# New durations and weights in the plan that orders a gated-attention and long-convolution kernel

## The chip, the core and the metric

The kernel runs on one core of a Trainium2 chip. The core has a matrix engine (TensorE, PE in the profile), a vector engine (VectorE, DVE), a scalar engine (ScalarE, ACT), a general engine (GpSimd, POOL) and a sync engine (SP), which here only issues transfers. Each engine takes its own instructions in the order in which the program has them and waits on semaphores for the others. The metric is the device time of one execution in microseconds (us); the median of the runs shown is what the change is held against.

## The reference

There are 8 batches of 3136 positions with 256 channels; `z` has 64 channels. Cut to what matters:

```python
scores = z @ z.T / S                    # S = 3136, per batch
attn = np.maximum(scores, 0.0) ** 2
x = u * (attn @ v)                      # 3136 x 256
x1, x2, x3 = split(x @ w_proj, 3)       # 256 channels each
X2 = rfft(x2, n=S); H = rfft(filter_fft, n=S)
y = x1 * irfft(X2 * H, n=S) * x3        # circular convolution along the positions
out = y @ w_out
```

So each batch has a squared-relu attention without a softmax, whose scores are symmetric, a gate `u`, three projections, a convolution over all 3136 positions by Fourier transform, a gate by `x1 * x3`, and a last projection.

## The kernel before

**The work of a batch.** The 3136 positions are 25 row tiles of 128 (the last has 64) and seven column chunks of 512, 512, 512, 512, 512, 256 and 320 (`CHUNKS`, line 24). For a chunk and a pair of row tiles, two score matmuls of 64 rows write the two halves of one of three pairs of PSUM banks (`ps_s`); they lie on the upper and the lower 64 rows of the array and run at the same time. ACT applies the relu (line 1672) into an SBUF tile `R_t`, DVE (line 1681) or ACT (line 1679) squares it into `A_t`, and "weighing" matmuls of 128 rows add `v` times `A_t` into two more banks, `ps_o0` and `ps_o1`, over all row tiles of the chunk. Since the scores are symmetric, the tiles of a later chunk are not computed twice: SP transposes them into `M` tiles (line 1610). When a chunk is done, DVE multiplies each of the two accumulators by `u` and the scale into `xT_t` (function `xe`, line 1722). That takes two instructions per accumulator, one for each half of 64 positions in a tile. The matmuls with `wp` then make `x1`, `x3` and `x2`; DVE's product of `x1` and `x3`, again in two instructions (`ev3`, line 1059), is kept as `gate_t`.

**The convolution.** A Fourier transform of 3136 = 64 x 49 points is made by matmuls in two stages with a trip through DRAM between them: `dft1` (line 889) writes `spec`, `load_spec` and `forward` read it again, DVE multiplies with the filter's transform `H`, `inverse` goes back through DRAM, and `add_end` (line 1224) does the last stage, the product with `gate_t` into `yT_t` (line 1252), the matmul with `wo`, a copy into `ost_t` and the store. This work of one batch is laid among the attention of the next.

**The plan.** No loop fixes the order of the instructions. The kernel makes a list of tasks, each with an estimated duration for every engine that may run it, its dependencies and the buffers it takes, and the class `Plan` (line 160) runs a clock over them: whichever engine can start a task first gets it, and the instructions are emitted in that order. Only the order reaches the chip; a task's estimated times do not. The estimates are `c_act`, `c_dve` and `c_pe` (lines 44 to 57), linear in the number of elements.

TensorE's tasks stand in queues: `S` for scores, `W` for weighing, `FA`, `FB` and `FZ` for projections, transforms and ends (called fill-in here). `pick_pe` (line 247) chooses. If scores are next and a run of them is already going, it goes on when the next pair of banks is free within `STAY`. Otherwise it wants two or three pairs free (three if the weighing that is ready is worth over `AMPLE`); while they are not, weighing may be taken, and fill-in too when the ready weighing is worth more than `BACKLOG` (line 29). Between weighing and fill-in a credit decides: each weighing task adds `PACE` (line 25), each fill-in task takes its duration away, and with a positive credit fill-in comes first, but only while `queued`, the work that ACT and DVE have waiting, is under `FULL` (line 37). The clock in `go` (line 309) adds a fixed time at every change from scores to other matmuls and back, since they use the array at different heights. For squares, `pick` (line 287) takes the engine that the clock says ends first, DVE being the first choice.

Of the kernel before, what the change touches and what calls it, by code (L numbers as in the profile page):

```python
# [21 lines left out]
KR = 2 * N2  # L22
KC = 100
CHUNKS = (512, 512, 512, 512, 512, 256, 320)
PACE = 0.6
HOLD = 3
DELAY = 4
GROUP = 1
BACKLOG, AMPLE, STAY = 2.0, 4.0, 0.1
LATE_PUT, LATE_LOAD, LATE_TURN, LATE_C, LATE_D2 = 3.0, 1.0, 1.5, 2.5, 1.0  # L30
SPEC_LAG = 1
LATE_F = 6.0
# [1 line left out]
FINAL = (0, 2, 4, 6, 1, 3, 5)  # L34
ZP, ZL = 0, 0.0
MOST = 3
FULL = 3.0
YIELD = 1.0
REACH = 2
INF = float("inf")  # L40
ISSUED = "issued"


def c_act(n):
    return 0.055 + n * 0.000833


def c_dve(n):
    return 0.068 + n * 0.00104
# [6 lines left out]
def c_pe(*ns):  # L56
    return sum(n / 2400 + 0.003 for n in ns)
# [102 lines left out]
class Plan:  # L160
# [86 lines left out]
    def pick_pe(self):  # L247
# [31 lines left out]
        order = ["S"]  # L279
        order += ["FA", "FB", "W", "FZ"] if self.credit > 0 and self.queued(t) < FULL else ["W", "FA", "FB", "FZ"]  # L280
        for k in order:
# [27 lines left out]
    def go(self):  # L309
        while True:  # L310
            got = []
            x = self.pick_pe()
            if x:
                got.append((x[0], 0, x[1], "PE", x[2]))
            for i, e in enumerate(self.pend):
                x = self.pick(e)
                if x:
                    got.append((x[0], i + 1, x[1], e, None))
            if not got:
                break  # L320
            start, _, task, e, k = min(got, key=lambda g: g[:2])
            if k:
                self.queues[k].remove(task)
                if (k == "S") != (self.mode == "S") and self.mode:
                    start += 0.11
                self.mode = k
                if k == "W":
                    self.credit = min(self.credit + PACE, 2.0)
                elif k != "S":
                    self.credit = max(self.credit - task.cost["PE"], -2.0)  # L330
            self.run(task, e, start)
        left = sum(len(q) for q in self.queues.values()) + sum(len(q) for q in self.pend.values())
        assert not left, f"{left} tasks left over"
# [3 lines left out]
def kernel(  # L337
# [60 lines left out]
    xT_p = Pool("xT", 8, [P, 2, 512], BF16)  # L398
# [93 lines left out]
    def on(engine, emit, cost, deps=(), takes=(), **kw):  # L492
        return job(None, lambda e: emit(), {engine: cost}, deps, takes, **kw)
# [13 lines left out]
    def both(n, first="ACT"):  # L507
        a, d = c_act(n), c_dve(n)
        return {"ACT": a, "DVE": d} if first == "ACT" else {"DVE": d, "ACT": a}
# [151 lines left out]
    for i, (t0, t1) in enumerate(zip(z_cuts, z_cuts[1:])):  # L661
        step_ = -(-(t1 - t0) // -(-(t1 - t0) // 8))
        for g0 in range(t0, t1, step_):
# [15 lines left out]
            n = nt * dqk  # L679
# [171 lines left out]
    for i0 in range(0, NS, 8):  # L851
        n = min(8, NS - i0)
# [170 lines left out]
    def add_proj(b, c, xt, xt_tasks):  # L1023
        cw = CHUNKS[c]
        users = []
        gtasks = []
        puts = []

        kind, late = ("FZ", 2) if b == B - 1 else ("FA", 0)

        def to_gates():
            for nb in range(2):
                box = {}

                def mm1(nb=nb, box=box):
                    box["p"] = bank()
                    box["x"] = x1_p.tile()
                    for k in range(2):
                        matmul(
                            box["p"][:, :cw], wp16[:, k, ds(nb * P, P)], xt["t"][:, k, :cw],  # L1040
                            start=(k == 0), stop=(k == 1),
                        )

                def ev1(e, box=box):
                    box["made"] = copy(e, box["x"][:, :cw], box["p"][:, :cw])

                def mm3(nb=nb, box=box):
                    box["p3"] = bank()
                    gates[b, c, nb] = g_p.tile()
                    for k in range(2):  # L1050
                        matmul(
                            box["p3"][:, :cw], wp16[:, k, ds((4 + nb) * P, P)], xt["t"][:, k, :cw],
                            start=(k == 0), stop=(k == 1),
                        )

                def ev3(nb=nb, box=box):
                    for h, w in halves(c):
                        g, p, x = (by_half(y, h, w) for y in (gates[b, c, nb], box["p3"], box["x"]))
                        got = nc.vector.tensor_tensor(g[:, ::-1] if h == 0 else g, p, x, ALU.mult)  # L1059
                        made.setdefault((b, c, nb), []).append(has_read(got, p, [box["made"]]))  # L1060

                a = pe(kind, mm1, c_pe(cw, cw), xt_tasks, [one_slots, x1_p.slots])
                if late and c in AFTER:
                    put_back.append(a)
                e1 = job(None, ev1, both(cw), [a], prio=late)
                e1.frees.append((a, 0))
                a3 = pe(kind, mm3, c_pe(cw, cw), [*xt_tasks, a], [one_slots, g_p.slots])
                e3 = on("DVE", ev3, c_dve(cw), [a3, e1], prio=late)
                e3.frees += [(a3, 0), (a, 1)]
                users.extend([a, a3])  # L1070
                gtasks.append((a3, e3))

        def to_spectrum():
            t0, n = T0[c], len(tiles[c])
            at = 0
            while at < n:
                nt = min(2, n - at)
                box = {}

                def mm2(at=at, nt=nt, box=box):  # L1080
                    box["p"] = bank()
                    box["x"] = x2_p.tile()
                    for k_ in range(nt):
                        for k in range(2):
                            matmul(
                                box["p"][:, ds(k_ * D, D)], xt["t"][:, k, ds((at + k_) * P, P)],
                                wp16[:, k, ds(D, D)], start=(k == 0), stop=(k == 1),
                            )

                def ev2(e, nt=nt, box=box):  # L1090
                    copy(e, box["x"][:, 0 : nt * D], box["p"][:, 0 : nt * D])

                a = pe("FA", mm2, c_pe(*[D] * (2 * nt)), xt_tasks, [one_slots, x2_p.slots])
                e2 = job(None, ev2, both(nt * D), [a])
                e2.frees.append((a, 0))
                users.append(a)
                puts.append(
                    dft1(
                        "FA", lambda box=box, nt=nt: box["x"][:, 0 : nt * D], t0 + at, nt, D1[b % 2],
                        [e2, t1_done], (a, 1), late=LATE_PUT * (b < B - 1),  # L1100
                    )
                )
                at += nt

        if b == B - 1 and c == NC - 1:
            to_spectrum()
            to_gates()
        else:
            to_gates()
            to_spectrum()  # L1110
        return users, puts, gtasks
# [225 lines left out]
    u_tasks = {}  # L1337
# [161 lines left out]
    w_first, w_last = {}, {}  # L1499
# [137 lines left out]
    for gi, g in enumerate(groups):  # L1637
        deps = []
        for un in g:
            b, c, k = un  # L1640
# [12 lines left out]
            for x in more:  # L1653
                weigh_short(*x)

        costs = [c_pe(CHUNKS[un[1]]) for un in g]
        extra = sum(c_pe(CHUNKS[c]) for _, c in more)
        st = pe("S", sg, sum(costs) + extra, deps, [pair_slots] * len(g))
        tails[gi] = st
# [1 line left out]
        for i, un in enumerate(g):  # L1661
            b, c, k = un
            cw = CHUNKS[c]
            pair = plans[b, c][k][1]
            rows, n = P, len(pair)
# [19 lines left out]
                "ACT", relu, c_act(n * cw), [(st, -sum(costs[i + 1 :]) - extra)], [R_p.slots], prio=0  # L1685
            )
            r_.frees.append((st, i))
            how = {"DVE": c_dve(n * cw)} if (b, c) == (0, 0) and k > 1 else both(n * cw, "DVE")
            q_ = job(None, sq, how, [r_], [A_p.slots], prio=1)
            q_.frees.append((r_, 0))  # L1690
            if c == NC - 1 and last or gi == len(groups) - 1:
# [15 lines left out]
            if last:  # L1707
                chunk_w[b, c] = [w_first[dh][0] for dh in range(2)], [w_last[dh] for dh in range(2)]
                xt = {}
                evs = []  # L1710
                for dh in range(2):

                    def xe(dh=dh, b=b, c=c, cw=cw, xt=xt):
                        if dh == 0:
                            xt["t"] = xT_p.tile()
                            if cw % P:
                                nc.vector.memset(xt["t"][:, :, cw : cw + N1], 0.0)
                        for h, n in halves(c):
                            x, f = by_half(xt["t"][:, dh], h, n), by_half(full[b, c, dh], h, n)
                            ut = uT[b, c][:, 0:n, dh, ds(h * N1, N1)]  # L1720
                            x = x[:, ::-1] if h == 0 else x
                            nc.vector.scalar_tensor_tensor(x, f, inv_s2, ut, ALU.mult, ALU.mult)  # L1722

                    x_ = on(
                        "DVE", xe, c_dve(cw), [w_last[dh], u_tasks[b, c], *((d, ISSUED) for d in evs)], [xT_p.slots] if dh == 0 else [], prio=-1
                    )
                    evs.append(x_)
                    x_.frees.append(w_first[dh])
# [45 lines left out]
    for gi, got in ends_at.items():  # L1774
        for b, c in got:
            q_, un, _ = short[b, c]
# [39 lines left out]
```

## Time and profile before

| | us |
|---|---|
| median of 3 runs | 1019.09 |
| lowest and highest run | 1015.51, 1020.16 |
| the profiled execution | 1017.42 |
| its span, first to last instruction | 1015.6 |
| PE busy | 980.1 (97%) |
| ACT busy | 882.6 (87%) |
| DVE busy | 821.6 (81%) |
| POOL busy | 188.3 (19%) |

The granted clock of TensorE was 0.998 over the span. The costliest groups are ACT's relus, 528 with 473.0 us; the weighing matmuls, 2128 with 480.4 us; DVE's squares, 334 with 366.5 us; and ACT's squares, 194 with 184.4 us. In the profile's lists of groups a row gives line, engine, operation, output and input tiles with their shapes, the count, then busy time and mean duration, and after the second bar the idle time of the engine just before these instructions and what ended it. In the timeline a row begins with its start and its length; equal neighbours are merged, and a bracket tells of idle time before the first. Matmuls overlap, because each is recorded from its issue to its modelled end; their starts say more than their lengths.

### The profile page before, as it was taken

To read this page: it belongs to the slowest core of one execution; us is meant where nothing else is said; L and a number is where in the kernel's file an instruction comes from. 1 tells how busy PE (TensorE), PEld (TensorE's weight loads), DVE (VectorE), ACT (ScalarE), POOL (GpSimd) and SP (SyncE) were. 2 spreads that over 40 slices of the span, in tenths; PEclk is the share of its full clock that TensorE was granted. 3 is DMA by queue.
4 is the path that set the end of the run, shared out by engine and by line. 5 is a ranking of instruction groups with operands and counts; after the bars stand their busy time and mean duration, and the time that the engine had idled before them with its cause. 6 is when DMAs were issued, how large, how long until landed. Compare 5 with 4: busy or idle time off the path is not lost. (4 is left out here: it accounts for less than half of the span.)

```text
span 1015.6 us, 17745 instructions
## 1 busy us (share of the span) xinstructions
PE 980.1 (97%) x6046; PEld 493.1 (49%) x6046; DVE 821.6 (81%) x1440; ACT 882.6 (87%) x1247; POOL 188.3 (19%) x401
## 2 busy tenths in 40 slices
PE   6999999999999999999999999999999999999986
PEld 2344644446444554445544464444644455544664
DVE  7977779877789787897789878887788977898674
ACT  5877899987989889888999898999888989998884
POOL 5142311123111310222012131112201132000000
PEclk9999999999999999999999999999999999999999
DMA  9699878888678799888988789696888979978756
GB/s 169 127 181 171 157 137 147 170 177 184 139 155 171 139 181 207 163 151 149 208 187 167 140 182 210 129 186 133 179 193 155 191 130 170 213 165 172 126 183 210
DMA packets 331770, 170.18 MB, mean 168 GB/s; under 512 B 241160, under 2 KB 306504, under 8 KB 331680
## 3 DMA queue, kind: packets, MB, share of 16 engines
q1 hardware_dynamic: 303952, 138.09, 63.0%
q0 software_dynamic: 27728, 30.97, 20.8%
q8 instruction: 47, 0.77, 0.3%
q14 instruction: 43, 0.35, 0.1%
HBM read 90.26 MB, written 53.35 MB: 141 GB/s over the span
## 5 line engine op out<-in xcount | busy, mean ns | idle before, releaser
L1672 ACT ACTIVATE R_t<-ps_s 128x1024 f32<-128x1024 f32 (+3 forms) x528 | 473.0, 932 | 71.0 <-PE ps_s L465 52.9
L465 PE MATMUL ps_o_t<-A_t,v_t 128*128 128x512 bf16 (+4 forms) x2128 | 480.4, 355 | 4.1 <-DVE A_t L1681 3.3
L1681 DVE TENSOR_TENSOR A_t<-R_t 128x1024 bf16<-128x1024 f32 (+3 forms) x334 | 366.5, 1114 | 113.0 <-ACT R_t L1672 112.2
L465 PEld LDWEIGHTS <-v_t 128*128 128x128 bf16 (+1 forms) x2826 | 253.5, 98 | 265.0 <-issue 65.3
L1679 ACT ACTIVATE A_t<-R_t 128x1024 bf16<-128x1024 f32 (+4 forms) x194 | 184.4, 955 | 2.5
L465 PE MATMUL ps_s<-zT_t 64*128 64x512 bf16 (+2 forms) x1064 | 152.6, 356 | 4.1 <-ACT s_t L498 1.7
L548 POOL COPY tick<-xT_t 1x1 bf16<-1x1 bf16 x54 | 13.8, 256 | 729.3 <-DVE xT_t L1722 713.2
L465 PE MATMUL ps_s<-xT_t,wp 128*128 128x512 bf16 (+2 forms) x430 | 102.6, 352 | 2.7 <-DVE xT_t L1722 1.3
L498 ACT ACTIVATE x_t<-ps_s 128x512 bf16<-128x512 f32 (+2 forms) x148 | 79.6, 573 | 25.4 <-PE ps_s L465 17.7
L1722 DVE SCALAR_TENSOR_TENSOR xT_t<-ps_o_t,uT_t 128x256 bf16<-128x256 f32 (+2 forms) x224 | 76.3, 382 | 21.3 <-PE ps_o_t L465 16.4
L465 PEld LDWEIGHTS <-zT_t 64*128 64x128 bf16 (+1 forms) x1081 | 44.8, 95 | 97.0 <-issue 78.6
L1158 DVE TENSOR_TENSOR xh<-xh,H 100x1024 bf16<-100x1024 bf16 x120 | 80.9, 685 | 3.0 <-ACT xh L498 2.2
L465 PE MATMUL ps_o_t<-M_t,v_t 128*128 128x512 bf16 (+2 forms) x352 | 82.2, 353 | 0.0
L1059 DVE TENSOR_TENSOR gate_t<-ps_s,x_t 128x256 bf16<-128x256 f32 (+2 forms) x214 | 71.1, 383 | 12.9 <-PE ps_s L465 11.0
L465 PEld LDWEIGHTS <-wp 128*128 128x128 bf16 x448 | 42.5, 97 | 45.7 <-issue 8.9
L539 POOL DMA_DIRECT2D un_t<-in_u_dram x112 | 59.9, 557 | 9.8 <-issue 5.7
L1252 DVE TENSOR_TENSOR yT_t<-ps_s,gate_t 128x512 bf16<-128x512 f32 (+2 forms) x97 | 58.2, 623 | 3.1 <-PE ps_s L465 2.6
L558 POOL DMA_DIRECT2D v_t<-in_v_dram x112 | 59.5, 554 | 6.0 <-issue 1.7
L465 PE MATMUL ps_s<-wp,xT_t 128*128 128x256 bf16 x398 | 56.4, 272 | 0.4 <-DVE gate_t L1059 0.2
L465 PE MATMUL ps_s<-wo,yT_t 128*128 128x256 bf16 (+1 forms) x366 | 54.2, 273 | 1.3 <-DVE yT_t L1252 0.9
L498 ACT ACTIVATE s_t<-ps_s 128x512 bf16<-128x512 f32 (+1 forms) x79 | 45.2, 587 | 9.4 <-PE ps_s L465 4.3
L498 ACT ACTIVATE xh<-ps_s 100x512 bf16<-100x512 f32 (+1 forms) x90 | 51.8, 611 | 1.6 <-PE ps_s L465 1.4
(148 smaller groups left out, 842.3 us busy)
## 6 DMA issues: line engine op xcount, KB each, us to landing
out_dram<-ost_t SPq DMA_DIRECT2D x66, 256.0 KB
spec<-s_t SPq DMA_DIRECT2D x96, 128.0 KB
spec_in_t<-spec SPq DMA_DIRECT2D x28, 392.0 KB
spec<-gs_t SPq DMA_DIRECT2D x28, 392.0 KB
v_t<-in_v_dram POOLq DMA_DIRECT2D x80, 128.0 KB, 4.1
un_t<-in_u_dram POOLq DMA_DIRECT2D x80, 128.0 KB, 4.5
conv_in_t<-spec SPq DMA_DIRECT2D x33, 256.0 KB
out_dram<-ost_t SPq DMA_DIRECT2D x19, 128.0 KB
```

Source lines behind the costliest of these rows:

```text
L465: wrote(nc.tensor.matmul(o, *args, **kw), o)
L498: got = nc.scalar.activation(out_, in_, AF.Copy)
L539: nc.gpsimd.dma_start(out=t[ds(j * N1, N1), lo - t0 : hi - t0, :], in_=x[:, n2 : n2 + hi - lo, :])
L548: nc.gpsimd.tensor_copy(tick[:], xt["t"][0:1, 1, 0:1])
L558: nc.gpsimd.dma_start(out=t[ds(j * N1, N1), ds(v_at(a), (b - a) * D)], in_=r[:, n2 + a - lo : n2 + b - lo, :].rearrange("p t d -> p (t d)"),)
L1059: got = nc.vector.tensor_tensor(g[:, ::-1] if h == 0 else g, p, x, ALU.mult)
L1158: nc.vector.tensor_tensor(x[:, 1 - i], x[:, 0], h, ALU.mult)
L1252: got = nc.vector.tensor_tensor(yb["y"][:, dh, 0:w], p, gates[b, c, dh][:, 0:w], ALU.mult)
L1672: has_read(nc.scalar.activation(blocks(box["R"], n, cw)[:rows], p, AF.Relu), p)
L1679: nc.scalar.activation(a, r, AF.Square)
L1681: nc.vector.tensor_tensor(a, r, r, ALU.mult)
L1722: nc.vector.scalar_tensor_tensor(x, f, inv_s2, ut, ALU.mult, ALU.mult)
```

## The change

Durations: the estimate of a DVE product of two instructions, for `xT` and for the gates, rises by 0.064 us. A square on ACT rises by 0.039. Each score matmul rises by 0.008. The time added at a change between scores and other matmuls falls from 0.11 to 0.095. Weights: `PACE` falls from 0.6 to 0.55 and `BACKLOG` from 2.0 to 1.0, and `FULL` becomes infinite, so that the condition on `queued` always holds. `INF` moves up in the file, and lines behind it stand one further down. The instructions themselves are written as before.

```diff
+INF = float("inf")
-PACE = 0.6
+PACE = 0.55
-BACKLOG, AMPLE, STAY = 2.0, 4.0, 0.1
+BACKLOG, AMPLE, STAY = 1.0, 4.0, 0.1
-FULL = 3.0
+FULL = INF
...
                 if (k == "S") != (self.mode == "S") and self.mode:
-                    start += 0.11
+                    start += 0.095
...
-                e3 = on("DVE", ev3, c_dve(cw), [a3, e1], prio=late)
+                e3 = on("DVE", ev3, c_dve(cw) + 0.064, [a3, e1], prio=late)
...
-        costs = [c_pe(CHUNKS[un[1]]) for un in g]
+        costs = [c_pe(CHUNKS[un[1]]) + 0.008 for un in g]
...
-            how = {"DVE": c_dve(n * cw)} if (b, c) == (0, 0) and k > 1 else both(n * cw, "DVE")
+            how = {"DVE": c_dve(n * cw)} if (b, c) == (0, 0) and k > 1 else {"DVE": c_dve(n * cw), "ACT": c_act(n * cw) + 0.039}
...
-                        "DVE", xe, c_dve(cw), [w_last[dh], u_tasks[b, c], *((d, ISSUED) for d in evs)], [xT_p.slots] if dh == 0 else [], prio=-1
+                        "DVE", xe, c_dve(cw) + 0.064, [w_last[dh], u_tasks[b, c], *((d, ISSUED) for d in evs)], [xT_p.slots] if dh == 0 else [], prio=-1
```

More of the change, by code (lines that the diff above doesn't have):

```diff
@@ L36 @@
 MOST = 3
-FULL = 3.0
+FULL = INF
 YIELD = 1.0
 REACH = 2
-INF = float("inf")
 ISSUED = "issued"
```

## The prediction

> **What bounds the kernel now.** I read the page's first two parts, then the timeline of TensorE alone, then the waits, then the stretches of time, and last the timeline around the final load of the spectrum.
>
> ```profile
> PE 980.1 (97%) x6046; PEld 493.1 (49%) x6046; DVE 821.6 (81%) x1440; ACT 882.6 (87%) x1247; POOL 188.3 (19%) x401
> PE   6999999999999999999999999999999999999986
> ```
>
> TensorE (PE) is busy in every slice but the first and the last two. "Busy" says little of pipelined matmuls, so I go by their starts:
>
> ```profile
> 499.56 1.89 PE L465 MATMUL ps_o_t<-A_t,v_t 128*128 128x512 bf16 x8
> 501.39 0.82 PE L465 MATMUL ps_s<-zT_t 64*128 64x512 bf16 x6
> 502.14 1.04 PE L465 MATMUL ps_o_t<-A_t,v_t 128*128 128x512 bf16 x4
> ```
>
> Eight matmuls of 512 columns begin at 499.56 and the next group at 501.39, 1.83 us later; an undisturbed matmul of 512 columns follows the one before it after 0.215 us (the commonest interval in this timeline; 0.109 for 256 columns, 0.135 for 320, 0.055 for 128), so eight are 1.72, and about 0.1 is left over. The six score matmuls are 64 rows high and run two at a time: three times 0.215 is 0.645, the next group begins 0.75 after them, and again 0.1 is left. That remainder, 0.095 in the median, stands at every change between matmuls of 64 and of 128 rows. With these intervals the built order of before needs 909.1 us of streaming and 404 changes x 0.095 = 38.4. Before the first matmul lie 4.7 us and after the last one 8.1. Together that is 960.3 of the span's 1015.6; 55.3 us are waits: 8.8 in the first 25 us, 10.2 in the last 50, some 36 in between. **So the end is set by TensorE's order and by its small waits**, and no other engine has a share to give.
>
> ```profile
> PEld L465 <- DVE xT_t L1722: 11.9, 25, 1.1
> PE ps_o_t L465 <- DVE A_t L1681: 3.3, 8, 0.6
> PE ps_o_t L465 <- DVE xT_t L1722: 2.1, 5, 0.8
> PE ps_s L465 <- ACT s_t L498: 2.0, 2, 1.7
> PE ps_s L465 <- DVE gate_t L1059: 1.4, 4, 0.7
> ```
>
> Columns: who waits for whom, us in all, times, longest. The largest of these is the product that makes `xT` (two DVE instructions at L1722): the weight loads stood 11.9 us for it, the matmuls themselves, whose modelled ends cover a part, 2.1 here. By starts it is between: 7.2.
>
> ```profile
> 30.00:955.00 925.00, 912.73 (x5581) 452.76 (x5580) 758.90 (x1298) 826.63 (x1154) 174.64 (x368) 1.00 0.85 167
> 967.00:974.40 7.40, 6.41 (x59) 4.39 (x58) 6.12 (x15) 4.83 (x9) 0.00 (x0) 1.00 0.48 141
> ```
>
> Stretches: length, then busy time of PE, weight loads, DVE, ACT and POOL, granted clock, DMA. In the body ACT works 826.6 of 925 us and DVE 758.9: neither is full, and the clock is 1.00.
>
> ```profile
> 966.59 0.49 PE L465 MATMUL ps_s<-x_t,T 128*128 128x512 bf16 x2
> ...
> 969.86 0.34 SPq L928 DMA_DIRECT2D spec_in_t<-spec  x1
> ...
> 973.73 0.90 PE L465 MATMUL ps_s<-wo,yT_t 128*128 128x256 bf16 x4 [0.45 <-DVE yT_t L1252]
> 974.46 0.60 PE L465 MATMUL ps_s<-spec_in_t,S 98*100 98x256 bf16 x4
> ```
>
> At the tail the last first-stage transform (966.59) is copied, stored, loaded again (issue 969.86) and used at 974.46: 7.9 us of transfers, which fill-in matmuls worth 5.8 us cover in part.
>
> **The change part by part.** The 6046 matmuls stay the same; five instructions net go from DVE to ACT. What changes is the order that the plan makes, so I compare the two built orders.
>
> (1) Balance. DVE gets 7 more squares of 1024 columns (1.220 us each) and ACT 7 fewer (1.068), ACT 16 more `gs_t` copies (0.613) and DVE 16 fewer (0.685); with the smaller moves, each at its row's mean, ACT gains 1.4 us and DVE loses 3.1, of 882.6 and 821.6. On engines that are not full I take nothing; bounds -1.4 and +1.4.
>
> (2) Start. TensorE's order is the same up to its first 21.4 us of work, which in the trace ends near 35.9 us; ACT's first 27 and DVE's first 73 instructions are the same. The 8.8 us of waits of the first 25 us stay: 0.
>
> (3) Changes of height: 426 instead of 404. 22 x 0.095 = +2.1 us, all of it on TensorE. The Trainium skill, page "TensorEngine Tiling (Array Packing)", section "Key Properties", says that a change of tiling mode drains TensorE; that speaks against this change, and the 0.095 at each change agrees with it. By the 166 ns that its page "TensorE: Matmul & The Clock Gate", section "Single matmul latency", gives as the fixed part of a lone warm matmul, the term would be +3.7 and the forecast 1.6 us later, as an estimate; the row is this kernel's own and decides.
>
> (4) Tail. In the changed order 4.3 us of fill-in stand between that last transform and the first use of the spectrum, not 5.8: eight matmuls of 512 columns (projections to gates, 8 x 0.215 = 1.7) now stand ahead of the transform, two of 256 columns moved in (0.2). The wait is one of transfers (issue at 969.86, use 4.6 us later), so work moved ahead of it delays the whole tail: +1.5. Bounds: 0, if the fill-in had itself been late (its last group waited 0.45 for `yT`), and +1.7. Behind it the order of all engines has the same steps, and the distances to the final loads are equal (5.4 us at the least in both).
>
> (5) Waits in the body. For every result that TensorE needs from ACT or DVE I took the distance in the built order: matmul work, at the intervals above and 0.095 per change, between the last matmul that fed it and the first that needs it, or that overwrites the bank. Short distances wait. For each kind I chose the length at which the shortfalls of the old order add up to the wait measured in the trace by starts (intervals over 25 ns too long, 40 to 955 us: 25.0 in all), and took the new order's shortfalls at the same length:
> `xT` to the projections, 0.96 us: 2.8 becomes 1.7. `xT` to the next chunk's accumulators, 1.33: 4.5 becomes 0.8. Gates (L1059), 1.23: 1.4 to 0.6. DVE squares, 2.84: 2.5 to 1.1. ACT squares, 3.54: 0.9 to 2.4. Relu to other work on its bank, 1.33: 3.7 to 2.8; to scores, 1.79: 0.3 to 1.3. ACT copies to scores, 1.28: 4.7 to 5.9; to other work, 0.99: 1.0 to 1.2. DVE copies, 1.12: 1.4 to 2.2. `yT`: 0.0 to 0.2. Together 23.2 becomes 20.2: -3.0.
> This fits the edit: products of two instructions get 0.064 us more in the plan (0.600 to 0.664 for 512 columns, where the trace has 2 x 0.417 and in the timeline 0.75 for both), so they are asked for later. What is late next are ACT's copies ahead of scores, since with `BACKLOG` at 1.0 scores and fill-in crowd more. ACT squares were short at two places only, so their length is the least certain; without them the term is -4.5. Bounds: -9.6 (all waits for `xT`, gates and ACT squares go) and +5, from the same stretch: as many waits as came off `xT` and the gates come back on copies.
>
> No transfer in the body comes nearer: a mirrored tile is used 12.2 us of work or more after its scores before, 12.9 after; a spectrum of an earlier batch 14.9 and 13.8, where the tail's wait shows that 7.9 are enough.
>
> Sum: 2.1 + 1.5 - 3.0 = +0.6. The profiled execution took 1017.42 us (span 1015.6, 1.8 around it), so 1018.0. That execution lies 1.7 below the median of 1019.09 and inside 1015.51 to 1020.16; about 0.5%, 5 us, is what a measurement of this kernel can tell from none.
>
> **The rivals.**
> Better match. If a plan whose durations are the chip's loses not single waits but a general mistrust, half of the 25.0 us go: -12.5 + 2.1 + 1.5 = -8.9, 1008.5. For it: four durations that are corrected (squares on ACT, two-instruction products, score matmuls, 0.110 to 0.095 per change) stand at 9.6 us of waits. Against: distances to copies and relus, two fifths of the waits, aren't longer in the new order.
> Other waits, as many. The order is redrawn and the body's waits remain 25: 1017.4 + 2.1 + 1.5 = 1021.0. For it: the waits lie evenly, about 0.4 us in 10; against: `xT`'s distances are clearly longer.
> Bunching, the slower one. `FULL` at infinity takes away the brake that held back projections, spectra and ends while ACT and DVE had over 3 us of work queued. With the rows' durations laid where their inputs are ready in the order, the mean load of ACT and DVE exceeds a stretch of 10 us by 7.4 us in all before and by 15.5 after (40 to 900 us of TensorE's work). If each such excess becomes a wait, +8.1: 1026.1. Against: the worst stretch holds 11.8 us of work in 10, 1.8 too much, while the median weighing stands 6.7 us behind its scores and needs 2.8, so 3.9 are in reserve. It decides from where excesses adjoin and pass 3.9.
> No effect. The new values might have left the order as it was; but it differs from TensorE's 22nd us on.
>
> **How the numbers follow.** Forecast 1018.0, chance 0.45, own range 1013 to 1023. Better match 0.20. Redrawn 0.17. Bunching 0.18. Against 1019.09, faster by over 0.5% is below 1014.0: nearly all of the better match and a tenth of the forecast, 0.25. Slower is above 1024.2: most of the bunching and a little of the forecast and of the redrawn, 0.19. Same: 0.56. The range 1009 to 1026 reaches almost to both outer cases and holds the bounds of (3) to (5) but their last ends.
>
> **What would show it.** In the changed kernel's waits, weight loads standing for `xT` should fall from 11.9 to near 6, and `ACT` copies ahead of score matmuls should not fall; the interval at a change of height stays 0.095; between the last `x_t,T` and the first `spec_in_t,S` there are still 7.5 to 8 us, with TensorE idle for some 3.5 instead of 2. I'm wrong if the sum of waits in the body leaves 18 to 28 us, if DVE has stretches full for 20 us with TensorE standing behind squares, or if the tail's wait shrinks.

## The result and the profile after

The changed kernel takes 1021.06 us in the median of 13 runs (1019.16 to 1026.08), the kernel before 1017.42 in the median of as many on the same chip: a ratio of 1.0036, 95% interval 1.0022 to 1.0049. It is 3.7 us slower. (The three runs shown before the prediction had a median of 1019.09; the ten added ones brought it down by 1.7.) The time lies in the predicted range, 3 us above the forecast of 1018.0; but the forecast was no change that could be seen, and the change is a loss. The profiled execution after took 1019.36 us, its span is 1017.6; it is among the quickest of the 13.

The page of the changed kernel, its busy time per engine and, in 40 slices, TensorE's busy share and granted clock:

```profile
PE 975.4 (96%) x5957; PEld 493.6 (49%) x6046; DVE 820.0 (81%) x1435; ACT 884.1 (87%) x1252; POOL 189.0 (19%) x401
...
PE   6999999999999999999999999999999999999985
...
PEclk9999999999999999999999999999999999999998
```

89 of the 6046 matmul records are missing here, so PE's busy time is not smaller than before; the weight loads are complete. ACT gained 1.5 us and DVE lost 1.6, and neither is fuller in any way that counts. New is the 8 at the end of the clock.

The waits of the changed kernel, first of weight loads, then of matmuls, then of ACT (who waits for whom, us in all, times, longest):

```profile
PEld L466 <- DVE xT_t L1723: 8.2, 21, 0.7
...
PE ps_s L466 <- ACT ost_t L499: 2.7, 4, 1.1
PE ps_s L466 <- ACT x_t L499: 2.5, 7, 0.4
...
ACT ost_t L499 <- DMA out_dram<-ost_t: 4.7, 4, 1.9
```

`xT` costs less, 8.2 instead of 11.9, as the new estimate of its product would have it. The last line is the one that grew most: ACT stood four times, 4.7 us in all, at a copy into an output buffer `ost_t` until a store of that buffer had landed. In the trace before that happened once, for 1.1 us. TensorE's waits for those copies are the 2.7 us above them.

What one such wait looks like. First ACT in the changed kernel, then the chain of what released it (start, us, what):

```profile
725.07 1.94 ACT L1673 ACTIVATE R_t<-ps_s 128x1024 f32<-128x1024 f32 x2 [0.44 <-PE ps_s L466]
727.28 0.60 ACT L499 ACTIVATE ost_t<-ps_s 128x512 f32<-128x512 f32 x1 [0.27 <-DMA out_dram<-ost_t]
729.78 1.08 ACT L499 ACTIVATE ost_t<-ps_s 128x512 f32<-128x512 f32 x2 [1.90 <-DMA out_dram<-ost_t]
730.75 1.95 ACT L1673 ACTIVATE R_t<-ps_s 128x1024 f32<-128x1024 f32 x2
```

```profile
721.40 0.28 SPq L1312
...
721.73 7.94 DMA out_dram<-ost_t
...
```

The copy at 727.28 is the only one of the short chunk of 256, the next the first of another chunk. That one could have begun at 727.9; it began at 729.78, when a store issued at 721.7 had landed, 7.9 us after its issue. ACT works in order, so the relu at 730.75 is late too, and with it the score banks. The same happens 122 us earlier, in the batch before. The SP queue shows why the store was out so late; first the changed kernel, then the kernel before at the same place of its batch:

```profile
594.42 0.53 SPq L941 DMA_DIRECT2D conv_in_t<-spec  x1
595.05 1.18 SPq L1392 DMA_TRANSPOSE zT_t<-zd_t  x1
596.39 1.97 SPq L1348 DMA_TRANSPOSE uT_t<-un_t  x1
598.45 2.70 SPq L1312 DMA_DIRECT2D out_dram<-ost_t  x4
...
608.14 1.11 SPq L1312 DMA_DIRECT2D out_dram<-ost_t  x2
```

```profile
600.09 1.20 SPq L1311 DMA_DIRECT2D out_dram<-ost_t  x2
604.39 0.37 SPq L903 DMA_DIRECT2D spec<-s_t  x1
604.88 1.75 SPq L1311 DMA_DIRECT2D out_dram<-ost_t  x2
...
610.69 1.12 SPq L1311 DMA_DIRECT2D out_dram<-ost_t  x2
```

Before, the stores of three chunks go out in pairs 4.8 and 5.8 us apart. In the new order two chunks end close together (their `wo` matmuls begin at 592.6 and 595.5). The first one's copies are done at 594.5, but its stores stand behind a load and two transposes until 598.4, and both chunks' four stores leave in one row. At 604.4 the third and the fourth chunk come, 12 `wo` matmuls in one group, and need both buffers again. The last of the four stores lands 6.9 us after its issue here (600.57 to 607.41) and 7.9 in the next batch, and the fourth chunk's copy waits for it. The plan counts 3.8 us from issue to landing on a free bus (1.2 + 4 x 0.45 + 0.8, from its constants), so it took both chunks to be free of any wait. That is about the usual time: each store marks its landing in the trace by 16 semaphore updates, and by these the median of the 92 stores is 3.7 us before and 3.6 in the changed kernel. Single stores take up to 8.1 and 8.4; the pairs of the kernel before that are shown above took 4.4 and 5.3, 3.5 and 4.0. By the Trainium skill, page "DMA: Bandwidth & Descriptors", section "Anatomy of one DMA — SWDGE (gpsimd) path", a transfer issued by GpSimd takes about 2.0 us and its bytes at 436 GB/s, which as an estimate makes 3.2 us for the 512 KB of a chunk. These stores are issued by SP and were not alone; the trace has 6.9 and 7.9 here, and decides.

The tail, TensorE in the changed kernel (start, us, line, operation, idle before):

```profile
966.77 0.49 PE L466 MATMUL ps_s<-x_t,T 128*128 128x512 bf16 x2
...
974.21 0.81 PE L466 MATMUL ps_s<-spec_in_t,S 98*100 98x256 bf16 x5 [0.35 <-ACT ost_t L499]
...
976.17 0.42 PE L466 MATMUL ps_o_t<-un_t,S 98*100 98x512 bf16 x1 [0.72 <-DMA un_t<-spec]
...
977.59 0.85 PE L466 MATMUL ps_s<-xh,TZ 100*98 100x256 bf16 x3
```

and stretches of the changed kernel (length, then busy time of PE, weight loads, DVE, ACT and POOL, granted clock, DMA share, GB/s):

```profile
967.00:974.40 7.40, 5.86 (x56) 4.01 (x55) 5.06 (x12) 4.55 (x9) 0.00 (x0) 1.00 0.44 129
974.02:977.43 3.41, 2.09 (x11) 1.02 (x11) 1.44 (x3) 2.99 (x8) 0.00 (x0) 1.00 0.81 226
977.40:980.80 3.40, 3.37 (x14) 2.86 (x14) 2.20 (x4) 1.56 (x3) 0.00 (x0) 0.50 1.01 387
```

The trip of the spectrum is no longer than before (966.77 to 974.21 is 7.4 us, 7.9 before). Then the clock drops to 0.50 for 3.41 us: the three matmuls of 256 columns at 977.59 take 0.64 us until the next group instead of 0.33.

### The profile page after: what moved, and what is told of

It reads as the page before. It is cut to its first block, busy times and chain, and to the rows that moved or that the text cites. A ratio compares the mean times of both kernels' runs of the same rounds, so it can differ in the third digit from the quotient of the medians.

```text
span 1017.6 us, 17693 instructions
## 1 busy us (share of the span) xinstructions
PE 975.4 (96%) x5957; PEld 493.6 (49%) x6046; DVE 820.0 (81%) x1435; ACT 884.1 (87%) x1252; POOL 189.0 (19%) x401
## 4 chain that ended last, share of the span: by engine, by line
PE 75%; DVE 10%; ACT 6%; DMA 5%; issue 3%; SPq 1%; ACTq 0%; DVEq 0%
PE ps_o_t L466 43%; PE ps_s L466 32%; DVE A_t L1682 3%; ACT R_t L1673 3%; DMA out_dram<-ost_t 2%; DVE xh L1159 2%; ACT A_t L1680 1%; ACT x_t L499 1%; DVE x_t L503 1%; DVE gate_t L1060 1%; DVE xT_t L1723 1%; DMA un_t<-spec 1%; DMA ost_t<-in_z_dram 1%; DVE yT_t L1253 0%; DMA A_t<-spec 0%
## 5 line engine op out<-in xcount | busy, mean ns | idle before, releaser
L466 PE MATMUL ps_o_t<-A_t,v_t 128*128 128x512 bf16 (+4 forms) x2061 | 471.9, 354 | 9.9 <-DVE A_t L1682 3.0
L1682 DVE TENSOR_TENSOR A_t<-R_t 128x1024 bf16<-128x1024 f32 (+3 forms) x341 | 373.1, 1111 | 107.4 <-ACT R_t L1673 106.5
L466 PEld LDWEIGHTS <-v_t 128*128 128x128 bf16 x2826 | 253.7, 98 | 261.2 <-issue 67.6
L1680 ACT ACTIVATE A_t<-R_t 128x1024 bf16<-128x1024 f32 (+3 forms) x187 | 177.8, 957 | 2.5
L466 PE MATMUL ps_s<-zT_t 64*128 64x512 bf16 (+2 forms) x1064 | 155.3, 357 | 5.6 <-ACT ost_t L499 2.4
L499 ACT ACTIVATE gs_t<-ps_s 98x512 bf16<-98x512 f32 (+1 forms) x99 | 59.1, 617 | 3.4 <-PE ps_s L466 3.1
L499 ACT ACTIVATE xh<-ps_s 100x512 bf16<-100x512 f32 (+1 forms) x93 | 54.1, 618 | 2.0 <-PE ps_s L466 1.8
L466 PE MATMUL ps_s<-wo,yT_t 128*128 128x256 bf16 (+1 forms) x358 | 51.7, 273 | 1.3 <-DVE yT_t L1253 0.9
```

Of the source, the lines that this page charges most:

```text
L466: wrote(nc.tensor.matmul(o, *args, **kw), o)
L499: got = nc.scalar.activation(out_, in_, AF.Copy)
L1680: nc.scalar.activation(a, r, AF.Square)
L1682: nc.vector.tensor_tensor(a, r, r, ALU.mult)
```

## The experiments

Two measures are used. "Body waits" is the sum of step (5) of the prediction: intervals between matmul starts over 25 ns too long, from 40 to 955 us; it is given where the trace has all its matmul records. "Last 50 us" is the account of all waits there. Ratios are against the kernel before, run on the same chip beside them.

**Four runs on where the loss sits.** They were made before the output buffers were suspected; their theories put the loss into the tail, its clock, or bunched work.

```diff
# dur_only: the new durations, the old weights
-PACE = 0.55
+PACE = 0.6
-BACKLOG, AMPLE, STAY = 1.0, 4.0, 0.1
+BACKLOG, AMPLE, STAY = 2.0, 4.0, 0.1
-FULL = INF
+FULL = 3.0
# weights_only: the kernel before with the three new weights
# late_old: the changed kernel; from the last batch's first scores on
...
+            if g[0][0] == B - 1:
+                PACE, BACKLOG, FULL = 0.6, 2.0, 3.0
# warm_after: the changed kernel with 8 more matmuls in the tail's gaps
+                    for _ in range({0: 3, 4: 3}.get(j, 0) if final else 0):
+                        matmul(box["p"][:, :], ident[:, :], wp16[:, 0, 0:512], start=True, stop=True)
...
+                        for _ in range(2 if final and j == 0 else 0):
+                            matmul(box["p"][:, :], ident[:, :], wp16[:, 0, 0:512], start=True, stop=True)
```

> The corrected durations alone, with the old weights 0.6, 2.0 and 3.0. Built order: 426 changes of height; the last first-stage transform ends at 910.2 us of TensorE's work, and 9.4 us of fill-in follow, more than the 7.7 us that the transfers take. Distances in the body give 20.7 us of waits against 23.1 before. Theory A: the tail starts only 0.3 us later than before and stays filled, so 0.3 - 2.4 = -2.1 us, ratio 0.998, with the clock at 1.0 up to the last matmul. Theory C (body waits redrawn, 22 more changes of height): +2.1, ratio 1.002 or more.

> The new weights 0.55, 1.0 and infinite with the old durations. Built order: 412 changes of height; the last first-stage transform ends at 912.8 us of TensorE's work, 5.5 us of fill-in follow; distances give 18.7 us of waits in the body against 23.1. Theory A: +1.2 for the tail, -4.4 in the body: -3.2 us, ratio 0.997. Theory D, bunching: without the brake on fill-in, ACT and DVE are overrun and the weights are what made the kernel slower: +3 us or more, ratio over 1.003.

> The changed kernel whose three weights go back to 0.6, 2.0 and 3.0 when the scores of the last batch begin. In its built order the last first-stage transform ends 914.1 us into TensorE's work (changed kernel 915.4, before 911.6), 5.3 us of fill-in follow it (4.5 and 5.8), changes of height are 426 as in the changed kernel. Theory A, the loss is in the tail: the order of batches 0 to 6 keeps the smaller waits, the tail begins 1.3 us earlier and is better filled, so the time falls by 1.3 us and by what the half clock costs, to 1018 against 1021 for the changed kernel (ratio to before 1.000 to 1.001). Theory C, the loss is in the body and redrawn: nothing is won, ratio 1.003 to 1.005.

> The changed kernel with its order kept and eight idle-filling matmuls of 512 columns added in the tail (three ahead of the first transform of the last spectrum, three ahead of the fifth, two ahead of the first inverse; their result is overwritten). Theory A, the clock: in the changed kernel's profile TensorE's granted clock is 0.5 from 977.43 to 980.85, behind a stretch in which it stood in waits about half of the time, and matmuls there take twice as long. If that is a cause of the loss, the fillers keep the clock at 1.0 up to the last matmul, the mean clock rises from 0.995 to 0.998 and the time falls by 1 to 2 us against the changed kernel, to about 1.002 of the kernel before. Theory B, order alone: the half clock lies in a wait for data anyway; the clock stays up but the time is the same or up to 1.7 us (8 x 0.215) longer, 1.0036 to 1.005.

| | median us | ratio | 95% interval |
|---|---|---|---|
| `dur_only` | 1015.11 | 0.9984 | 0.9972 to 0.9996 |
| `weights_only` | 1032.51 | 1.0146 | 1.0124 to 1.0169 |
| `late_old` | 1018.97 | 1.0018 | 1.0007 to 1.0029 |
| `warm_after` | 1020.94 | 1.0033 | 1.0020 to 1.0046 |

The durations alone are a gain, the weights alone a loss of 15 us. `dur_only` is where theory A had it (0.998), but not by A's mechanism: A had the clock at 1.00 up to the last matmul, and in its trace it is 0.50 from 976.3 to 979.7 us. `weights_only` is far from A's 0.997. `warm_after` keeps the clock at 1.00 up to 1015.2 of its 1019.7 us and shows no gain, which speaks for B (the half clock lies where TensorE has to wait anyway); its interval just reaches A's 1.002. `late_old` was expected at 1.000 to 1.001: the last batch's order carries about a half of the loss by the medians, not all. The new weight `BACKLOG` can be left out of account: the changed kernel with `BACKLOG` at 2.0 has the same order on every engine.

The trace of `weights_only` showed the cause at its plainest. ACT, then TensorE, then two stretches, of that kernel:

```profile
378.23 0.60 ACT L498 ACTIVATE ost_t<-ps_s 128x512 f32<-128x512 f32 x1 [4.42 <-DMA out_dram<-ost_t]
```

```profile
374.77 0.39 PE L465 MATMUL ps_s<-zT_t 64*128 64x512 bf16 x2
378.88 0.58 PE L465 MATMUL ps_s<-zT_t 64*128 64x512 bf16 x1 [3.71 <-ACT ost_t L498]
379.39 1.78 PE L465 MATMUL ps_o_t<-A_t,v_t 128*128 128x320 bf16 x6
```

```profile
374.00:377.20 3.20, 1.16 (x9) 0.50 (x7) 1.68 (x3) 0.00 (x0) 0.00 (x0) 1.00 1.30 224
377.30:384.10 6.80, 5.22 (x19) 2.27 (x18) 3.13 (x7) 3.94 (x7) 0.00 (x0) 0.50 0.70 168
```

ACT waits 4.4 us for a store, TensorE 3.7 us behind it, and then the clock stands at a half for 6.8 us: six matmuls of 320 columns take 1.57 us to the next group instead of 0.81. Such waits hold DVE and ACT 10.4 us in this trace, and half clock comes three times ahead of the end.

**A quarter of the stores, and `FULL` alone.** The three `thin` kernels leave out the other three quarters of the output; their orders are those of the kernels they are made from. `undo_full` has an order of its own.

```diff
# thin_before, thin_after, thin_weights
-                        out=r[:, n2 : n2 + hi - lo, :], in_=ob["o"][ds(j * N1, N1), i0 : i0 + hi - lo, :]
+                        out=r[0:16, n2 : n2 + hi - lo, :], in_=ob["o"][ds(j * N1, 16), i0 : i0 + hi - lo, :]
# undo_full: the changed kernel
-FULL = INF
+FULL = 3.0
```

> The kernel before, which stores 16 of every 64 rows of its output (the other 48 rows are left out); the order on TensorE, ACT, DVE and POOL is that of before. It is the base for the next two. The trace of before shows no copy to the output buffer that waits for a store of it, so both theories expect little: ratio 0.997 to 1.000, the rest of the gain being the last store of the program.

> The changed kernel with the same quarter of the stores; its order is that of the changed kernel. Theory S (the new weights bring two copies to an output buffer closer together than its store takes, ACT stands at its head, and TensorE and at times its clock follow): the 2.9 us that the changed kernel loses beyond changes of height, tail and body distances go, and the ratio is 1.0005 to 1.0015 above that of the kernel before with a quarter of the stores. Theory O (the order on TensorE alone loses them, whatever the stores do): it stays 1.003 to 1.004 above it. Under S the profile has no copy to the output buffer that waits for a store.

> The new weights on the old durations, with a quarter of the stores. In its trace with all stores ACT stands five times, 10.4 us in all, at a copy to an output buffer until a store has landed, and the clock is at a half three times. Theory S: most of the 15 us go; the ratio is 0.996 to 1.003 above (times) that of the kernel before with a quarter of the stores, and the half clock before the tail does not appear. Theory O: 1.012 to 1.016, as with all stores.

> The changed kernel with FULL at 3.0 again, PACE and BACKLOG new. If FULL is the weight that costs: near the kernel with new durations and old weights, 0.998 to 1.0005. By the tail and the distances alone (last transform 0.3 us later than before, waits in the body 1.5 more, as worked out from its built order): 1.002. If PACE costs: 1.003 to 1.004, as the changed kernel.

`thin_before` 1011.98 us (0.9938, more of a gain than expected; behind the last matmul its span has 4.6 us instead of 8.1), `thin_after` 1010.39 (0.9922), `thin_weights` 1017.03 (0.9995). Against `thin_before` the changed order is now 1.6 us faster instead of 3.7 slower, and the new weights alone are 5.0 slower instead of 15. Each of these ratios carries about 0.002, so the 1.6 us are no sure gain. Theory O is out (it had 3 to 4 us and 12 to 16 above `thin_before`), and S is the nearer one, though both results lie outside its ranges, the order's 1.6 us below `thin_before` instead of 0.5 to 1.5 above and the weights at 1.005 times instead of at most 1.003. Lighter stores relieve every other transfer as well. `undo_full`: 1017.12 us, 0.9995 (0.9981 to 1.0010). By the two ratios `FULL` at infinity costs 4.2 us. Yet with `FULL` at 3.0 the copies wait for stores as well, DVE and ACT for 6.1 us in all; ACT's part of it in `undo_full`:

```profile
ACT ost_t L499 <- DMA out_dram<-ost_t: 5.7, 3, 3.5
```

**A third output buffer.** Its room comes from two `xT` buffers that the order never needs; the plan goes on counting two and eight, so that the order on all engines is unchanged.

```diff
-    xT_p = Pool("xT", 8, [P, 2, 512], BF16)
+    xT_p = Pool("xT", 6, [P, 2, 512], BF16); xT_p.slots = Slots(8)
-    o_p = Pool("ost", 2, [P, 4, D], F32)
+    o_p = Pool("ost", 3, [P, 4, D], F32); o_p.slots = Slots(2)
```

> The changed kernel with three buffers for output rows instead of two (the room comes from two spare xT buffers; the planner still counts two and eight, so the order on every engine is that of the changed kernel). All stores are made. Theory S (a copy to an output buffer waits for the buffer's last store): the distance to before with a quarter of the stores was -1.6 us, with all of them +3.7; a third buffer takes the wait away and gives most of these 5.3 us back: ratio to before 0.998 to 1.0005, and no copy to the output buffer waits for a store. Rival L (a quarter of the stores was faster because all transfers had a lighter load): as the changed kernel, 1.003 to 1.004.

> The kernel before with the same third output buffer. S: TensorE stood 0.4 to 0.8 us for one such wait in its trace, so 0.9985 to 1.000. L: 1.000.

> New durations, old weights (0.9984 as it stood), with the third output buffer. S: DVE and ACT stood 5.3 us for stores there and TensorE 1.7 us behind them, so 0.996 to 0.9975. L: 0.998 to 0.999.

> Old durations, new weights (1.0146 as it stood, 5.0 us above before with a quarter of the stores), with the third output buffer. S: 1.003 to 1.006, and no half clock before the tail. L: 1.013 to 1.016.

| | two buffers | three buffers | 95% interval (three) |
|---|---|---|---|
| before | 1 | 0.9995 | 0.9983 to 1.0006 |
| changed kernel | 1.0036 | 0.9958 | 0.9942 to 0.9974 |
| new durations alone | 0.9984 | 0.9961 | 0.9942 to 0.9980 |
| new weights alone | 1.0146 | 1.0050 | 1.0031 to 1.0070 |

Rival L is out: all bytes are stored and 0.0078 of the changed kernel's time, 7.9 us, goes, and 9.8 of the weights' 15. S had put it at 5.3; it is more. It is also more than the wait itself shows in a trace: TensorE stood 2.7 us for copies into `ost_t` in the changed kernel, and 4.3 by starts in `late_old`. Where the rest comes off is not shown. In the traces with three buffers no copy waits for a store. ACT, and TensorE at the place shown above one batch earlier, in the changed kernel with three buffers:

```profile
602.73 1.94 ACT L1673 ACTIVATE R_t<-ps_s 128x1024 f32<-128x1024 f32 x2 [0.44 <-PE ps_s L466]
604.79 1.57 ACT L499 ACTIVATE ost_t<-ps_s 128x512 f32<-128x512 f32 x3
606.24 1.96 ACT L1673 ACTIVATE R_t<-ps_s 128x1024 f32<-128x1024 f32 x2
```

```profile
606.00 0.71 PE L466 MATMUL ps_o_t<-A_t,v_t 128*128 128x320 bf16 x4
606.64 0.60 PE L466 MATMUL ps_s<-zT_t 64*128 64x512 bf16 x3
607.18 0.99 PE L466 MATMUL ps_o_t<-A_t,v_t 128*128 128x320 bf16 x6
```

The three copies run in a row, and the three score matmuls too. The account of the two kernels with three buffers:

| us | before | changed |
|---|---|---|
| body waits | 23.2 | 16.2 |
| waits of the last 50 us | 10.2 | 12.4 |
| changes of height x 0.095 | 404: 38.4 | 426: 40.5 |
| span | 1013.1 | 1010.9 |

With two buffers the body waits were 25.0 before; `late_old`, whose order is the changed kernel's up to about 879 us, has 21.9, of them 4.3 for `ost_t`.

**The tail and the weights, once stores are out of the way.**

```diff
# ost3_late_old, ost3_undo_full, ost3_undo_pace: three buffers in late_old, undo_full
# and in the changed kernel with
-PACE = 0.55
+PACE = 0.6
```

> The changed kernel with a third output buffer and the old weights from the last batch's scores on. Theory T (the order of the tail costs by itself, as worked out from the place of the last transform, 1.3 us earlier here): 1.3 to 2 us faster than the changed kernel with the third buffer, which was at 0.9958, so 0.9935 to 0.9948. Rival S2 (the 2 us that this variant was faster by with two buffers were waits for stores): as that kernel, 0.995 to 0.997.

> The changed kernel with a third output buffer and FULL at 3.0. Theory F1 (FULL cost 4 us by bringing copies and stores together, and nothing else): by its built order its transform comes 3.5 us earlier in the tail and its waits in the body add 4.5, so about the changed kernel with the third buffer, 0.9955 to 0.9975. Rival F2 (FULL costs on TensorE itself): 4 us below that kernel as with two buffers, 0.991 to 0.9925.

> The changed kernel with a third output buffer and PACE at 0.6. The built order's tail and distances are within 0.6 us of the changed kernel's. If PACE has no share of its own: 0.995 to 0.9965. If it costs on TensorE: below 0.994.

`ost3_late_old` 1010.08 us, 0.9930 (0.9915 to 0.9946); `ost3_undo_full` 1010.03, 0.9929 (0.9912 to 0.9945); `ost3_undo_pace` 1013.24, 0.9956 (0.9939 to 0.9974). The tail's order costs 0.0028, 2.8 us, by itself (theory T had 1.3 to 2; each ratio carries 0.0016, so a difference of two some 2.3 us), and `PACE` nothing that can be seen. F1, that `FULL` costs through stores alone, falls: 0.0029 remain with the wait gone. But it is about what the tail's old order brings as well, and the waits of the last 50 us are 10.3 with `FULL` at 3.0 where they were 12.4. That `FULL` acts there is likely; a kernel with `FULL` changed in the body alone was not run. With `FULL` at 3.0 the third buffer is worth 6.7 us (0.9995 to 0.9929), nearly the 7.9 of the changed kernel, and with the new durations alone 2.3 (0.9984 to 0.9961). So it is not `FULL` alone that brings copies and stores together. That leaves `PACE`, alone or with the new durations, but the changed kernel with two buffers and `PACE` at 0.6 was not run, so this stays open. `ost3_late_old` and `ost3_undo_full` are the two fastest kernels here that write the whole output, 7 us below before.

**The plan told the truth about stores.** Two buffers again, and a later time at which the plan counts one as free.

```diff
+            s_.late += 3.5 if dst is o_p else 0.0
             s_.frees.append((o0, 1))
```

> The changed kernel with two output buffers, but the plan counts an output buffer as free 3.5 us later than it did. In the built order the work on TensorE between the last matmul of a chunk and the first of the chunk that takes its buffer is then 9.8 us or more (6.9 in the changed kernel, 10 of 44 under 9). The redrawn order has its last transform 2.0 us earlier and 4.6 us more of short distances to ACT and DVE. Theory S: 3.7 - 7.4 - 2.0 + 4.6 = -1.1 us against before, 0.997 to 1.000, and no copy waits for a store. Rival (the third buffer helped in some other way than by this wait): 3.7 - 2.0 + 4.6 = +6.3, 1.004 to 1.008.

> The same with FULL at 3.0: its two-buffer kernel was at -0.6 us; transform 1.2 us later, distances 3.9 more, stores 6.2 less. S: -1.7 us, 0.997 to 0.9995. Rival: +4.5, 1.003 to 1.006.

`late35_after` 1016.07 us, 0.9992 (0.9977 to 1.0007); `late35_undo_full` 1015.12, 0.9975 (0.9966 to 0.9984). Both as S has them, the rival's 1.004 and 1.003 lie outside. No copy waits for a store in either trace. SP still sends four stores in a row (of `late35_after`):

```profile
603.44 2.80 SPq L1312 DMA_DIRECT2D out_dram<-ost_t  x4
```

but the third chunk now comes later. The price is the new order's: in `late35_after` the body waits are 24.4, 6.7 of them for DVE's squares.

## Why the prediction was wrong

- **(1) and (2), balance and start: right.** ACT +1.5 (1.4 foreseen), DVE -1.6 (3.1 foreseen, of no weight); the waits of the first 25 us are 8.8 in both traces.
- **(3), changes of height, +2.1: right.** The trace of `ost3_after` has 426 changes, and the median of what one leaves over is 0.095 again, as in the changed kernel.
- **(5), waits in the body, -3.0: this step failed, in its last sentence.** "No transfer in the body comes nearer" was said of mirrored tiles and spectra; the store that must land before an output buffer is written again was not looked at. It is a transfer whose data nothing reads again, and ACT, not TensorE, waits for its end. It cost 7.9 us in the changed kernel's runs and 0.5 before: a term of +7.4 where the sum had none. The other part was undersized the other way: by the distances to ACT and DVE the body's waits should have fallen by 3.0; with the stores' wait gone they fell by 7.0 (23.2 to 16.2), inside the bound of 9.6. Both errors met in the trace, where the body of `late_old` shows 21.9, just the 25.0 - 3.0 of the step: by luck a trace with two buffers alone would have seemed to confirm it.
- **(4), tail, +1.5: right in kind, perhaps too small.** The runs have 2.8 with an uncertainty of some 2.3, the trace with three buffers 2.2. The bound of 1.7 was the work moved; left out was that the half-filled stretch behind it is followed by half clock, in the trace after as in that with three buffers. Keeping the clock up alone gave nothing back that could be seen, so whether anything is missing here, and what, stays open.
- **The sum.** 2.1 + 2.8 - 7.0 + 7.4 = 5.3 against 3.7 measured; the terms from runs carry some 2 us each, the 7.0 comes from one trace of each kernel, and the difference lies within that.
- **The rivals.** "Other waits, as many" named 1021.0, and 1021.06 came: waits that left `xT` did come back on copies, but on their buffers' stores, not on their distances; that the number fits is luck, since 7.0 went and 7.4 came. "Bunching" named a weight that does cost, `FULL`, but by excess work on ACT and DVE; with three buffers the body of the changed order waits less, not more, and the kernel is 4.3 us faster than before. For the new weights on the old durations it is not out: 5.0 us remain there with no copy waiting for a store. "Better match" foresaw 12.5 us off the body's waits; with the stores' wait gone 7.0 went, and the new durations alone give 4.0 us (0.9961).
- **Its signs.** `xT` from 11.9 to 8.2 rather than 6; ACT's copies ahead of scores did not fall; none of its signs of being wrong spoke of a store, and the body's waits of 21.9 stayed inside 18 to 28; the last transform to the spectrum took 7.4 us, just under the 7.5 to 8; TensorE idle there for 2.9 us (7.1 from the transform's end, less 4.2 of fill-in) rather than 3.5. So the tail's wait shrank by about 0.5, which it had named as a sign of being wrong.

## What to carry to other kernels

When an order changes, list for every buffer all that must end before it can be written again, the store that empties it included, and follow that store through its queue to its landing; a wait of this kind holds an in-order engine and everything queued behind it. Give the plan the landing time that the trace shows under load, not that of a free bus: with 3.5 us more in the plan the loss of 3.7 us was gone (0.8 faster, not to be told from none), and with one more buffer it became a gain of 4.3. A correction of durations and a change of weights in one edit can hide each other: here -1.6 and +15 alone, +3.7 together.

## What the hardware showed beyond this

The clock went to a half without a long idle stretch. In the tail of the changed kernel, TensorE was busy for 2.09 of the 3.41 us ahead of the drop, and the longest wait in its lines there is 0.72 us; the half clock then held for 3.41 us. In `weights_only` 3.7 us of idle time brought 6.8 us of it. The Trainium skill, page "TensorE: Matmul & The Clock Gate", section "HAM oscillation — how this bites in real kernels", gives as the rule no idle gaps over some 3.4 us; the second case fits it, the first shows that shorter gaps can do. Neither the busy share nor the longest wait decides it in these traces: in the tail of `ost3_dur` (three buffers, new durations) TensorE was busy for less, 1.92 of 3.41 us, with a wait of 0.90 us, and the clock stayed at 1.00 up to 1006.4 us.

```profile
989.26:992.67 3.41, 1.92 (x19) 1.24 (x18) 2.67 (x8) 0.85 (x2) 0.00 (x0) 1.00 0.94 262
```

And the last of four stores sent in a row behind transposes landed 6.9 and 7.9 us after its issue, while rows of four elsewhere in the same trace landed within 3.8 (943.3 us): four in a row are not slow by themselves.
